# Sparse attention with a routed feed-forward net: transposes of two tokens at once, copies between engines moved, end blocks in 64 columns

## The chip, the cores and the metric

The kernel runs on one core of one Trainium2 chip. A core has engines that work side by side, each through its own queue in order: TensorE (PE, matrix products and transposes, results to PSUM), VectorE (DVE), ScalarE (ACT), GpSimd (POOL) and SyncE (SP, which here only starts transfers). Sixteen DMA engines carry the transfers. The metric is the device time of one execution, in microseconds (us).

## What is computed

Four batches of eight heads with 768 positions and 64 dimensions go through block-sparse attention in blocks of 32 positions. The 3,072 rows that result are then routed to eight experts with 384 places each. The reference, cut to its core:

```python
mask = abs(blk_i - blk_j) <= 1                     # the neighbouring blocks
mask |= (blk_i == 0) | (blk_j == 0) | (blk_i == n_blocks - 1) | (blk_j == n_blocks - 1)
for qb in range(n_blocks):                         # 24 blocks, 3 drawn for each
    for kb in sampled_blocks[qb]:
        mask[32*qb:32*qb+32, 32*kb:32*kb+32] = True
attn = softmax(where(mask, q @ k.T / 8, -1e9))
x = (attn @ v) as rows of 8 heads x 64             # 3072 x 512
logits = x @ w_gate                                # 512 x 8
# all 24576 (token, expert) pairs from the highest logit down: a token goes to the
# first expert with a free place (384 each)
out[rows of e] = relu(x[rows of e] @ w1[e]) @ w2[e]
```

## The kernel before

The program has two parts, one after the other: `Attn` (lines 26 to 462) and `Moe`, whose planner with its own clock places routing and expert products. The change touches `Attn` alone. All numbers are 32-bit floats.

**Layout.** Keys and queries of a batch are needed with the dimension on the partitions: `T[b, "k"]` and `T[b, "q"]`, tiles of 128 x 4 x 768, where partition 64s + d of slice p holds dimension d of head 2p + s. `load_pair` brings them in as `st`, 96 partitions with four neighbouring tokens each, and `prep` (L130) turns them. One call turns two of the four tokens for both heads of a pair: eight products with the identity (L141), each with 64 columns of `st` as weights and 96 moving columns, into one PSUM tile `ptr` or `pT`, and one evacuation with the scale, on ACT (L147) or, for odd places among the first sixteen, on DVE (L149). The evacuation writes every fourth column of `T`. There are sixteen calls in a batch. In the traces a product of 32-bit floats counts as two matmul instructions, a transpose as one.

**Units.** The work of a batch is 24 units in pairs, one for each half s of the heads' partitions. "I" units (20 of them: u = 0 to 4, m, s) handle four middle blocks of queries, u's blocks 4u + 1 to 4u + 4, for two heads; "M" units (2) handle blocks 21 and 22 for four heads; "D" units (4) handle the end blocks, 23 and 0, which attend to all 768 positions. In a batch after the first one D pair comes first and the other after the units of u = 1; then come the rest, and M at the end.

**What a unit goes through.** `qk_pair` (L215) makes the scores of a pair into PSUM tiles `S` (L235; for I and M against gathered keys `kg`, for D against `kT`, four pieces of 32 query columns for every half). `sm_unit` (L237) takes the row minimum (L252, for D L244) and subtracts it (L253 on DVE, for D L247 on ACT). `tr_unit` (L256) transposes the scores (L266) and takes the exponential while it evacuates them (L267, ACT). `av_unit` (L273) multiplies with the value rows (L293 for I and M, from `vw` and `vz`; L280 for D, from `vn`), and `finish` (L298) divides by the sums on DVE. Then come three short tasks, one an iteration: `l1` transposes the attention rows (L342, L344), `l2` multiplies with the gate weights `wp`, padded to 32 columns, into four strips of experts by tokens (L351, L353), and `l3` transposes these (L357) and adds the strips up on DVE into the logits `lg` (L360).

**Gathers.** Each u has its own keys and values in one of two buffers. `gather_k` (L161) fills `kg[u % 2]` with copies: first and last block of the batch (u = 0 and 1 only; L168, L169), the neighbouring blocks (L173, L175, L176 on DVE, in later batches for u = 0 on POOL; L177, L178 on POOL) and the three drawn ones (L182, POOL, twelve copies). `gather_v` (L192) fetches the drawn value rows from DRAM with one indirect transfer for each block (L199, started by POOL) into `vz`, and copies the neighbouring rows from `vn` into `vw` on ACT (L195) and DVE (L202, L210, L212, and memsets L204, L207). `value_frame` (L184) brings the end blocks' rows by transfers of SP.

**Order.** `run` (L364) writes the order of all queues by hand, in a software pipeline. Iteration n issues, in this order: the scores of the pair n + 1 and n + 2 (when n is odd), the products with values of unit n - 3, one task, the transposes of the scores of unit n - 1, stores, then for unit n the softmax step, the gathers and loads that are due, and at the end one `prep` of the next batch. Gathers hang on the place i of a unit in its u:

```python
if i == 3 and u < 4:
    self.gather_k(b, u + 2)
if i == 2:
    self.gather_v(b, u + 1)
```

In M, `gather_k(b + 1, i)` makes both key buffers of the next batch, one for each M unit. `prep` uses the PSUM tile `px`, or, when a D unit is among the last four, one of the two buffers `pT` that the transposes use too.

Of the kernel before, what the change touches and what calls it, by code (L numbers as in the profile page):

```python
# [25 lines left out]
class Attn:  # L26
# [23 lines left out]
    def consts(self):  # L50
        nc, cst = self.nc, self.cst
        sb32 = self.sb.tensor.bitcast(I32)
        self.tab = cst.tile([128, NB, 3, 2], I32, name="tab")
        nc.scalar.dma_start(self.tab.rearrange("p n r w -> p (n r w)"),
                            bass.AP(tensor=sb32, offset=0, ap=[[0, 128], [1, 2 * NB * 3]]))
        self.tbl = cst.tile([128, NB, 3], I32, name="tbl")
        nc.vector.tensor_scalar(self.tbl, self.tab[:, :, :, 0], 0, NB - 1, op0=OP.max, op1=OP.min)
        self.kg = [cst.tile([128, HP, 4, 256], F32, name=f"kg{i}") for i in range(2)]
        self.vw = [cst.tile([128, 4, VR], F32, name=f"vw{i}") for i in range(2)]
        self.vz = [cst.tile([128, 4, VR], F32, name=f"vz{i}") for i in range(2)]  # L60
# [69 lines left out]
    def prep(self, b, p, nm, t, n=None, px=True):  # L130

        nc = self.nc
        if p == 0 and t == 0:
            self.T[b, nm] = self.qk.tile([128, HP, S], F32, name=nm + "T")
        ps = (self.px[:, 0:384] if px
              else self.pA.tile([128, 512], F32, name="pT")[:, 0:384])
        for h in range(2):
            for c in range(2):
                x = 64 * (2 * t + h)
                for s in range(2):  # L140
                    nc.tensor.matmul(ps[64 * s:64 * s + 64, 192 * h + 96 * c:192 * h + 96 * c + 96],  # L141
                                     self.st[b, p, nm][:, c, s, x:x + 64], self.ident[0:96, 0:96], start=True, stop=True)
        dst = self.T[b, nm][:, p].rearrange("d (r x) -> d x r", x=4)[:, 2 * t:2 * t + 2]
        src = ps.rearrange("d (x r) -> d x r", x=2)
        sc = 1.0 if nm == "k" else -0.125
        if n is None or n % 2 == 0:
            nc.scalar.activation(dst, src, AF.Copy, scale=sc)  # L147
        else:
            nc.vector.tensor_scalar(dst, src, sc, None, op0=OP.mult)  # L149
# [11 lines left out]
    def gather_k(self, b, u):  # L161
        nc = self.nc
        kg, kT = self.kg[u % 2], self.T[b, "k"]
        e = nc.gpsimd if b else nc.vector
        if u < 2:
            for g in range(4):
                s = 32 * ((g + 3) % 4)
                e.tensor_copy(kg[:, :, g, s:s + 32], kT[:, :, 0:32])  # L168
            e.tensor_copy(kg[:, :, :, 224:256], kT[:, :, None, S - BS:S].to_broadcast([128, HP, 4, BS]))  # L169
        e = e if u == 0 else nc.vector  # L170
        x = 128 * u
        for g in range(2):
            e.tensor_copy(kg[:, :, g, 32 * g:32 * g + 96], kT[:, :, x + 32 * g:x + 32 * g + 96])  # L173
        if u < 5:
            e.tensor_copy(kg[:, :, 2:4, 96:128], kT[:, :, None, x + 96:x + 128].to_broadcast([128, HP, 2, 32]))  # L175
            e.tensor_copy(kg[:, :, 2:4, 0:32], kT[:, :, None, x + 128:x + 160].to_broadcast([128, HP, 2, 32]))  # L176
            nc.gpsimd.tensor_copy(kg[:, :, 2, 64:96], kT[:, :, x + 64:x + 96])  # L177
            nc.gpsimd.tensor_copy(kg[:, :, 3, 32:64], kT[:, :, x + 160:x + 192])  # L178
        pv = self.sampled(u, ET.Pool)
        for g in range(len(self.blocks(u))):  # L180
            for r in range(3):
                nc.gpsimd.tensor_copy(kg[:, :, g, 128 + 32 * r:160 + 32 * r], kT[:, :, bass.ds(pv[3 * g + r] * BS, BS)])  # L182
# [9 lines left out]
    def gather_v(self, b, u):  # L192
        nc = self.nc
        vw, vz, vn = self.vw[u % 2], self.vz[u % 2], self.vn[b % 2].rearrange("p c h d -> p c (h d)")
        A = lambda o, i: nc.scalar.activation(o, i, AF.Copy)  # L195
        V = nc.vector.tensor_copy
        bl = self.blocks(u)
        for g in range(len(bl)):
            nc.gpsimd.indirect_dma_start(out=vz[0:96, g], out_offset=None, in_=self.vs[b],  # L199
                                         in_offset=bass.IndirectOffsetOnAxis(ap=self.vidx[:, bl[g]:bl[g] + 1], axis=0))  # L200
        A(vw[0:96, 0], vn[0:96, u])
        V(vw[32:64, 1], vn[32:64, u])  # L202
        if u == 0:
            nc.vector.memset(vw[0:32, 0], 0.0)  # L204
        if u == 5:
            A(vw[64:96, 1], vn[64:96, u])
            nc.vector.memset(vw[96:128, 1], 0.0)  # L207
            return
        A(vw[64:128, 1:3], vn[64:128, u, None].to_broadcast([64, 2, VR]))
        V(vw[0:32, 2], vn[0:32, u + 1])  # L210
        A(vw[96:128, 3], vn[96:128, u])
        V(vw[0:64, 3], vn[0:64, u + 1])  # L212


    def qk_pair(self, xs, js=(0, 1)):  # L215
# [6 lines left out]
        kg, bl = self.kg[u % 2], self.blocks(u)  # L222
        for j in js:
            for g in range(4):
                for s, x in enumerate(xs):
                    h = slice(64 * s, 64 * s + 64)
                    if kind == "D":
                        p, i = 2 * x["m"] + g // 2, (NB - 1, 0)[g % 2]
                        o, rhs = x["S"][j][32 * g:32 * g + 32, 0:384], kT[h, p, 384 * j:384 * j + 384]
                    else:  # L230
                        p, gi = (2 * x["m"] + j, g) if kind == "I" else (2 * j + g // 2, g % 2)
                        i = bl[gi]
                        o = x["S"][0][32 * g:32 * g + 32, 256 * j:256 * j + 256]
                        rhs = kg[h, p, gi]
                    nc.tensor.matmul(o, qT[h, p, BS * i:BS * i + BS], rhs, start=True, stop=True)  # L235
# [37 lines left out]
    def av_unit(self, x):  # L273
        nc, b, kind, u, m, s = self.nc, x["b"], x["kind"], x["u"], x["m"], x["half"]
        aT = x["aT"]
        if kind == "D":
            for n in range(6):
                for g in range(4):
                    h = 4 * m + 2 * (g // 2) + s
                    nc.tensor.matmul(self.px[32 * g:32 * g + 32, (D + 1) * s:(D + 1) * (s + 1)], aT[:, n, 32 * g:32 * g + 32],  # L280
                                     self.vn[b % 2][:, n, h], start=n == 0, stop=n == 5)
        else:
            if x["first"]:
                self.av = self.pV.tile([128, 512], F32, name="av")[:, 0:7 * (D + 1)].rearrange("p (h d) -> p h d", h=7)
# [13 lines left out]
    def finish(self, x):  # L298

        nc, b, kind, u = self.nc, x["b"], x["kind"], x["u"]  # L300
        av = self.av if kind != "D" else self.px[:, 0:2 * (D + 1)].rearrange("p (h d) -> p h d", h=2)
        n, f = {"I": (8, 7), "M": (4, 4), "D": (2, 2)}[kind]
        rc = self.wk.tile([128, 8, 1], F32, name="rc")
        nc.vector.tensor_scalar(rc[:, 0:f], av[:, 0:f, D:D + 1], 1e-9, None, op0=OP.add)
        if kind == "I":
            nc.vector.tensor_scalar(rc[:, 7], self.a7[:, D:D + 1], 1e-9, None, op0=OP.add)
        nc.vector.reciprocal(rc[:, 0:n], rc[:, 0:n])
# [30 lines left out]
        def l1():  # L338
# [4 lines left out]
            st["xT"] = self.wk.tile([128, HP, 128], F32, name="xT")  # L343
            nc.scalar.activation(st["xT"], ps, AF.Copy)  # L344

        def l2():
            ps = self.pA.tile([128, 512], F32, name="pT")
            xT = st["xT"]
            for p in range(HP):
                r = xT[:, p, :] if kind == "I" else xT[:, p - p % 2:p - p % 2 + 2, 64 * (p % 2):64 * (p % 2) + 64]  # L350
                nc.tensor.matmul(ps[32 * p:32 * p + 32, 0:128], self.wp[:, p, :], r, start=True, stop=True)  # L351
            st["LT"] = self.wk.tile([128, 128], F32, name="LT")
            nc.scalar.activation(st["LT"], ps[:, 0:128], AF.Copy)  # L353

        def l3():
            ps = self.pA.tile([128, 512], F32, name="pT")
            nc.tensor.transpose(ps[:, 0:128], st["LT"], self.ident)  # L357
            c = b * 6 + u
            for p0, n, c in ((0, 128, c),) if kind == "I" else ((0, 96, c), (96, 32, (c - 6) % NCH)):
                nc.vector.tensor_reduce(self.lg[p0:p0 + n, c], ps[p0:p0 + n, 0:128].rearrange(  # L360
                    "p (c e) -> p e c", c=4)[:, 0:E], axis=AX.X, op=OP.add)
        self.tasks += [l1, l2, l3]

    def run(self, start=None):  # L364
# [16 lines left out]
        flat = [(p, nm, t) for p in range(HP) for nm in "kq" for t in range(2)]  # L381
# [7 lines left out]
        for n in range(N + 3):  # L389
# [32 lines left out]
            if kind == "D":  # L422
# [5 lines left out]
                if i == (2 if b == 0 else 1):  # L428
                    self.gather_v(b, 0)
                    if b == 0:  # L430
# [5 lines left out]
            if kind == "I":  # L436
# [3 lines left out]
                if i == 3 and u < 4:  # L440
                    self.gather_k(b, u + 2)
# [735 lines left out]
```

## Time and profile before

| what | us |
|---|---|
| median of three runs | 786.71 |
| the runs | 780.67 to 787.73 |
| the profiled execution | 787.75 |
| its span, first to last instruction | 786.0 |
| DVE, ACT, POOL busy in the span | 485.1, 388.6, 398.6 |

The three runs differ by 0.9% between them. In the profile, a group names a line of the kernel, an engine, an operation and the tiles (`out<-in`), with the number of its instructions, then the busy time in us and the mean of one in ns, then the engine's idle time before them and what ended it. The view of waits gives, for each engine and line, what was waited for, with the total in us, the number of times and the longest. A line of the timeline gives the start in us from the span's start, the length in us, the engine, and what it did; neighbouring instructions of the same kind are merged, with their count. Windows give the busy time of each engine in a stretch. All instructions of the second part carry L541, which is a helper's line.

### The profile page before, as it was taken

How to read it: one execution, taken by the hardware profiler on the slowest of the kernel's cores; microseconds unless marked ns; L12 is line 12 of the kernel's file. 1: busy time of each engine (PE TensorE's matmuls, PEld its weight loads, DVE VectorE, ACT ScalarE, POOL GpSimd, SP SyncE). 2: the span in 40 equal slices, each digit the busy share in tenths (PEclk: the TensorE clock that was granted, in tenths of full speed). 3: DMA queues.
4: the chain of work that ended last, by engine and by line, in shares of the span. 5: the costliest groups of instructions: out<-in, count | busy, mean ns of one | idle time of the engine just before them, and what ended most of it. 6: DMA issues, size and time to landing. Idle time of an engine off the chain costs nothing. (4 is left out here: it accounts for less than half of the span.)

```text
span 786.0 us, 22329 instructions
## 1 busy us (share of the span) xinstructions
PE 636.2 (81%) x8736; PEld 481.6 (61%) x8736; DVE 485.1 (62%) x1730; ACT 388.6 (49%) x801; POOL 398.6 (51%) x741
## 2 busy tenths in 40 slices
PE   5768886788767978768767218999999999999997
PEld 5545663555544645545445117787878787889895
DVE  3447458473774657657695687868687878743120
ACT  2335553464534646435343427475757565644350
POOL 2275337336363254544440007575757676777671
PEclk9879998899987999869998558999999999999999
DMA  9945724845345673133321025434353535455411
GB/s 207 258 108 122 186 84 125 205 104 140 118 115 132 124 202 118 37 88 89 93 63 50 8 73 182 161 135 167 129 174 122 184 114 200 153 174 178 139 41 41
DMA packets 84865, 101.07 MB, mean 129 GB/s; under 512 B 30724, under 2 KB 61588, under 8 KB 84760
## 3 DMA queue, kind: packets, MB, share of 16 engines
q1 hardware_dynamic: 75104, 69.39, 30.5%
q0 software_dynamic: 9504, 30.18, 13.3%
q8 instruction: 69, 1.13, 0.7%
q14 instruction: 36, 0.29, 0.1%
q10 hardware_dynamic: 152, 0.08, 0.1%
HBM read 76.38 MB, written 18.98 MB: 121 GB/s over the span
## 5 line engine op out<-in xcount | busy, mean ns | idle before, releaser
L541 POOL TENSOR_TENSOR wlo<-raw,whi 128x512 fp32r<-128x512 f32 x128 | 161.6, 1288 | 58.0 <-ACT whi L541 57.3
L199 POOL DMA_INDIRECT vz<-vrows,vidx x88 | 84.1, 956 | 163.9 <-PE pT L293 130.1
L267 ACT ACTIVATE aT<-pT 128x512 f32<-128x512 f32 x88 | 52.6, 597 | 100.8 <-PE pT L266 100.7
L266 PE MATMUL pT<-ident,s 128*128 128x128 f32 x352 | 63.5, 306 | 33.6 <-DVE s L253 26.8
L182 POOL COPY kg<-kT 128x128 f32 x264 | 68.7, 308 | 24.3 <-issue 24.2
L541 PE MATMUL po<-whi,hh 128*128 128x512 f32 x192 | 77.4, 403 | 0.0
L541 PE MATMUL po<-whi,hl 128*128 128x512 f32 x192 | 77.0, 401 | 0.0
L252 DVE TENSOR_REDUCE mn<-S 128x2 f32<-128x512 f32 x88 | 59.8, 680 | 27.5 <-remote 15.7
L541 PE MATMUL po<-wlo,hh 128*128 128x512 f32 x192 | 76.5, 399 | 0.0
L541 ACT ACTIVATE whi<-raw 128x512 fp32r<-128x512 f32 x128 | 74.1, 621 | 0.1
L266 PEld LDWEIGHTS pT<-ident,s 128*128 128x128 f32 x352 | 43.5, 154 | 43.8 <-issue 30.6
L253 DVE TENSOR_TENSOR s<-S,mn 128x512 f32<-128x512 f32 x88 | 60.9, 692 | 10.8 <-PE pT L266 5.9
L293 PE MATMUL av<-vw,aT 128*32 128x65 f32 x1248 | 54.6, 244 | 14.0 <-issue 12.7
L293 PE MATMUL av<-vz,aT 128*32 128x65 f32 x1248 | 54.0, 239 | 14.0 <-issue 13.7
L235 PE MATMUL S<-kg,qT 64*32 64x256 f32 x1408 | 57.6, 401 | 3.9 <-issue 3.8
L541 DVE SCALAR_TENSOR_TENSOR hl<-ph,hh 128x384 fp32r<-128x384 f32 x64 | 35.3, 553 | 39.7 <-ACT hh L541 38.1
L541 PE MATMUL ph<-xhi,whi 128*128 128x384 f32 x256 | 58.4, 345 | 0.4 <-ACT xhi L541 0.3
L293 PEld LDWEIGHTS av<-vw,aT 128*32 128x32 f32 x1248 | 31.5, 118 | 43.9 <-issue 39.7
L541 PE MATMUL ph<-xhi,wlo 128*128 128x384 f32 x256 | 57.9, 343 | 0.0
L541 PE MATMUL ph<-xlo,whi 128*128 128x384 f32 x256 | 57.7, 342 | 0.0
L541 ACT ACTIVATE hh<-ph 128x384 fp32r<-128x384 f32 x64 | 31.2, 487 | 45.5 <-PE ph L541 42.4
L195 ACT ACTIVATE vw<-vn 96x520 f32<-96x520 f32 (+2 forms) x68 | 51.8, 762 | 1.0
(247 smaller groups left out, 1365.2 us busy)
## 6 DMA issues: line engine op xcount, KB each, us to landing
raw<-in_moe_w_dram SPq DMA_DIRECT2D x64, 512.0 KB
stk<-in_k_dram SPq DMA_DIRECT2D x32, 192.0 KB
stq<-in_q_dram SPq DMA_DIRECT2D x32, 192.0 KB
vn<-in_v_dram SPq DMA_DIRECT2D x24, 256.0 KB
xrows<-xt SPq DMA_DIRECT2D x20, 256.0 KB
vrows<-vn SPq DMA_DIRECT2D x9, 520.0 KB
vw<-vn SPq DMA_DIRECT2D x32, 65.0 KB
vz<-vn SPq DMA_DIRECT2D x8, 260.0 KB
```

Source lines behind the costliest of these rows:

```text
L182: nc.gpsimd.tensor_copy(kg[:, :, g, 128 + 32 * r:160 + 32 * r], kT[:, :, bass.ds(pv[3 * g + r] * BS, BS)])
L195: A = lambda o, i: nc.scalar.activation(o, i, AF.Copy)
L199: nc.gpsimd.indirect_dma_start(out=vz[0:96, g], out_offset=None, in_=self.vs[b], in_offset=bass.IndirectOffsetOnAxis(ap=self.vidx[:, bl[g] ...
L235: nc.tensor.matmul(o, qT[h, p, BS * i:BS * i + BS], rhs, start=True, stop=True)
L252: nc.vector.tensor_reduce(mn[:, 0:2], ps, axis=AX.X, op=OP.min)
L253: nc.vector.tensor_tensor(s.rearrange("p (j t) y -> p j (t y)", j=2), ps, mn[:, 0:2, None].to_broadcast([128, 2, 256]), op=OP.subtract)
L266: nc.tensor.transpose(ps[:, c, :], s[:, c0 + c, :], self.ident)
L267: nc.scalar.activation(aT[:, c0:c0 + w], ps[:, 0:w], AF.Exp, scale=-1.0 if n == 4 else 1.0)
L293: nc.tensor.matmul(o(self.col(x, j))[32 * g:32 * g + 32], aT[:, 2 * j + t, 32 * g:32 * g + 32], v[:, gi, h], start=t == 0, stop=t == 1)
L541: return f(*args, **kw)
```

## The change

Six edits, all in `Attn`.

- `prep(b, p, nm, s)` now turns all four tokens of one head: four transposes, each of 128 columns of `st` (two tokens), into 96 columns of the PSUM tile. Its two halves of 64 partitions hold the even and the odd tokens; ACT evacuates the first and DVE the second, each into every second column of `T`.
- The rows that DVE copied from `vn` to `vw` come by transfers of SP, in a new function `copy_v`, called one unit after `gather_v` (in the same unit for u = 0). The memsets go to POOL.
- The neighbouring keys go to POOL (L173) and ACT (L175, L176), also for u = 1 of the first batch; only its u = 0 stays on DVE.
- The end blocks' queries are put side by side by ACT into a new tile `qd`, so that scores and value products of D units take 64 columns at once.
- The logits come as tokens by experts straight from PE: the attention rows are the weights and the gate's eight columns move, added up over four products; ACT copies the result to `lg`. `l3`, its transpose and its addition on DVE go. `l1` of M puts its rows into the order that this needs.
- The sums in `finish` are kept in PSUM (`den`) and not in SBUF before their reciprocal.

```diff
-        wp = cst.tile([128, HP, 32], F32, name="wp")
-        nc.gpsimd.memset(wp, 0.0)
-        nc.gpsimd.dma_start(wp[:, :, 0:E], wg.rearrange("(c p) e -> p c e", p=128))
+        wp = cst.tile([128, HP, E], F32, name="wp")
+        nc.gpsimd.dma_start(wp, wg.rearrange("(c p) e -> p c e", p=128))
...
-        for h in range(2):
-            for c in range(2):
-                x = 64 * (2 * t + h)
-                for s in range(2):
-                    nc.tensor.matmul(ps[64 * s:64 * s + 64, 192 * h + 96 * c:192 * h + 96 * c + 96],
-                                     self.st[b, p, nm][:, c, s, x:x + 64], self.ident[0:96, 0:96], start=True, stop=True)
-        dst = self.T[b, nm][:, p].rearrange("d (r x) -> d x r", x=4)[:, 2 * t:2 * t + 2]
-        src = ps.rearrange("d (x r) -> d x r", x=2)
+        for c in range(2):
+            for t in range(2):
+                x = 192 * c + 96 * t
+                nc.tensor.transpose(ps[:, x:x + 96], self.st[b, p, nm][:, c, s, 128 * t:128 * t + 128], self.ident[0:96, 0:96])
         sc = 1.0 if nm == "k" else -0.125
-        if n is None or n % 2 == 0:
-            nc.scalar.activation(dst, src, AF.Copy, scale=sc)
-        else:
-            nc.vector.tensor_scalar(dst, src, sc, None, op0=OP.mult)
+        for z in range(2):
+            dst = self.T[b, nm][64 * s:64 * s + 64, p, z:S:2].rearrange("d (c r t) -> d c r t", c=2, t=2)
+            src = ps[64 * z:64 * z + 64].rearrange("d (c t r) -> d c r t", c=2, t=2)
+            if z == 0:
+                nc.scalar.activation(dst, src, AF.Copy, scale=sc)
+            else:
+                nc.vector.tensor_scalar(dst, src, sc, None, op0=OP.mult)
...
-        e = nc.gpsimd if b else nc.vector
+        e = nc.gpsimd if b or u else nc.vector
...
-        e = e if u == 0 else nc.vector
         x = 128 * u
         for g in range(2):
             e.tensor_copy(kg[:, :, g, 32 * g:32 * g + 96], kT[:, :, x + 32 * g:x + 32 * g + 96])
         if u < 5:
-            e.tensor_copy(kg[:, :, 2:4, 96:128], kT[:, :, None, x + 96:x + 128].to_broadcast([128, HP, 2, 32]))
-            e.tensor_copy(kg[:, :, 2:4, 0:32], kT[:, :, None, x + 128:x + 160].to_broadcast([128, HP, 2, 32]))
+            nc.scalar.activation(kg[:, :, 2:4, 96:128], kT[:, :, None, x + 96:x + 128].to_broadcast([128, HP, 2, 32]), AF.Copy)
+            nc.scalar.activation(kg[:, :, 2:4, 0:32], kT[:, :, None, x + 128:x + 160].to_broadcast([128, HP, 2, 32]), AF.Copy)
...
-        A(vw[0:96, 0], vn[0:96, u])
-        V(vw[32:64, 1], vn[32:64, u])
         if u == 0:
-            nc.vector.memset(vw[0:32, 0], 0.0)
+            nc.gpsimd.memset(vw[0:32, 0], 0.0)
+            A(vw[32:64, 0], vn[32:64, u])
+            A(vw[64:96, 0], vn[64:96, u])
+        else:
+            A(vw[0:96, 0], vn[0:96, u])
...
+    def copy_v(self, b, u):
+
+        vw, vn = self.vw[u % 2], self.vn[b % 2].rearrange("p c h d -> p c (h d)")
+        D = self.nc.sync.dma_start
+        D(vw[32:64, 1], vn[32:64, u])
+        if u < 5:
+            D(vw[0:32, 2], vn[0:32, u + 1])
+            D(vw[0:64, 3], vn[0:64, u + 1])
...
+        if kind == "D" and 0 in js:
+            p = 2 * xs[0]["m"]
+            for z, i in enumerate((NB - 1, 0)):
+                nc.scalar.activation(self.qd[:, p:p + 2, 32 * z:32 * z + 32], qT[:, p:p + 2, BS * i:BS * i + BS], AF.Copy)
         for j in js:
-            for g in range(4):
+            for g in range(2 if kind == "D" else 4):
...
-                        p, i = 2 * x["m"] + g // 2, (NB - 1, 0)[g % 2]
-                        o, rhs = x["S"][j][32 * g:32 * g + 32, 0:384], kT[h, p, 384 * j:384 * j + 384]
+                        p = 2 * x["m"] + g
+                        o, rhs = x["S"][j][64 * g:64 * g + 64, 0:384], kT[h, p, 384 * j:384 * j + 384]
+                        lhs = self.qd[h, p]
...
-                for g in range(4):
-                    h = 4 * m + 2 * (g // 2) + s
-                    nc.tensor.matmul(self.px[32 * g:32 * g + 32, (D + 1) * s:(D + 1) * (s + 1)], aT[:, n, 32 * g:32 * g + 32],
-                                     self.vn[b % 2][:, n, h], start=n == 0, stop=n == 5)
+                for g in range(2):
+                    nc.tensor.matmul(self.px[64 * g:64 * g + 64, (D + 1) * s:(D + 1) * (s + 1)], aT[:, n, 64 * g:64 * g + 64],
+                                     self.vn[b % 2][:, n, 4 * m + 2 * g + s], start=n == 0, stop=n == 5)
...
-                nc.tensor.matmul(ps[32 * p:32 * p + 32, 0:128], self.wp[:, p, :], r, start=True, stop=True)
-            st["LT"] = self.wk.tile([128, 128], F32, name="LT")
-            nc.scalar.activation(st["LT"], ps[:, 0:128], AF.Copy)
-
-        def l3():
-            ps = self.pA.tile([128, 512], F32, name="pT")
-            nc.tensor.transpose(ps[:, 0:128], st["LT"], self.ident)
-            c = b * 6 + u
+                nc.tensor.matmul(ps, xT[:, p], self.wp[:, p], start=p == 0, stop=p == HP - 1)
             for p0, n, c in ((0, 128, c),) if kind == "I" else ((0, 96, c), (96, 32, (c - 6) % NCH)):
-                nc.vector.tensor_reduce(self.lg[p0:p0 + n, c], ps[p0:p0 + n, 0:128].rearrange(
-                    "p (c e) -> p e c", c=4)[:, 0:E], axis=AX.X, op=OP.add)
-        self.tasks += [l1, l2, l3]
+                nc.scalar.activation(self.lg[p0:p0 + n, c], ps[p0:p0 + n], AF.Copy)
+        self.tasks += [l1, l2]
...
-                if i == 3 and u < 4:
-                    self.gather_k(b, u + 2)
+                if i == 3:
+                    self.copy_v(b, u + 1)
+                    if u < 4:
+                        self.gather_k(b, u + 2)
```

More of the change, by code (lines that the diff above doesn't have):

```diff
@@ L59, in consts @@
         self.vw = [cst.tile([128, 4, VR], F32, name=f"vw{i}") for i in range(2)]
+        self.qd = cst.tile([128, HP, 2 * BS], F32, name="qd")
         self.vz = [cst.tile([128, 4, VR], F32, name=f"vz{i}") for i in range(2)]
@@ L128, in value_rows, with prep @@
                                self.vn[b % 2][:, c:c + n].rearrange("p c h d -> p c (h d)"))
-    def prep(self, b, p, nm, t, n=None, px=True):
+    def prep(self, b, p, nm, s, n=None, px=True):
         nc = self.nc
-        if p == 0 and t == 0:
+        if p == 0 and s == 0:
             self.T[b, nm] = self.qk.tile([128, HP, S], F32, name=nm + "T")
@@ L195, in gather_v @@
         A = lambda o, i: nc.scalar.activation(o, i, AF.Copy)
-        V = nc.vector.tensor_copy
         bl = self.blocks(u)
@@ L301, in finish @@
         av = self.av if kind != "D" else self.px[:, 0:2 * (D + 1)].rearrange("p (h d) -> p h d", h=2)
+        den = self.avt[:, 480:488] if kind != "D" else self.px[:, 480:488]
         n, f = {"I": (8, 7), "M": (4, 4), "D": (2, 2)}[kind]
         rc = self.wk.tile([128, 8, 1], F32, name="rc")
-        nc.vector.tensor_scalar(rc[:, 0:f], av[:, 0:f, D:D + 1], 1e-9, None, op0=OP.add)
+        nc.vector.tensor_scalar(den[:, 0:f, None], av[:, 0:f, D:D + 1], 1e-9, None, op0=OP.add)
         if kind == "I":
-            nc.vector.tensor_scalar(rc[:, 7], self.a7[:, D:D + 1], 1e-9, None, op0=OP.add)
-        nc.vector.reciprocal(rc[:, 0:n], rc[:, 0:n])
+            nc.vector.tensor_scalar(den[:, 7:8], self.a7[:, D:D + 1], 1e-9, None, op0=OP.add)
+        nc.vector.reciprocal(rc[:, 0:n, 0], den[:, 0:n])
         r0 = b * S
@@ L342, in l1 @@
                 nc.tensor.transpose(ps[:, p, :], i_.rearrange("p a d -> p (a d)"), self.ident)
[L343 to L344 removed]
+            st["xT"] = xT = self.wk.tile([128, HP, 128], F32, name="xT")
+            if kind == "I":
+                nc.scalar.activation(xT, ps, AF.Copy)
+            else:
+                for a in (0, 2):
+                    nc.scalar.activation(xT[:, a:a + 2].rearrange("p o (z y) -> p z o y", z=2),
+                                         ps[:, a:a + 2].rearrange("p z (o y) -> p z o y", o=2), AF.Copy)
         def l2():
[L347 to L348 removed]
+            ps = self.pA.tile([128, 512], F32, name="pT")[:, 0:E]
+            xT, c = st["xT"], b * 6 + u
             for p in range(HP):
[L350 to L358 removed]
+                nc.tensor.matmul(ps, xT[:, p], self.wp[:, p], start=p == 0, stop=p == HP - 1)
             for p0, n, c in ((0, 128, c),) if kind == "I" else ((0, 96, c), (96, 32, (c - 6) % NCH)):
[L360 to L362 removed]
+                nc.scalar.activation(self.lg[p0:p0 + n, c], ps[p0:p0 + n], AF.Copy)
+        self.tasks += [l1, l2]
     def run(self, start=None):
@@ L380, in run @@
         N = len(units)
-        flat = [(p, nm, t) for p in range(HP) for nm in "kq" for t in range(2)]
+        flat = [(p, nm, s) for p in range(HP) for nm in "kq" for s in range(2)]
         for i, pr in enumerate(flat[:8]):
@@ L429, in run @@
                     self.gather_v(b, 0)
+                    self.copy_v(b, 0)
                     if b == 0:
```

11 lines of the change are left out of this document (5 added, 6 removed).

## The prediction

> **What bounds the kernel now.** First the page's head and its line of granted clock, then the busy times of three stretches.
>
> ```profile
> span 786.0 us, 22329 instructions
> PEclk9879998899987999869998558999999999999999
> ```
> ```profile
> 0.00:40.00 40.00, 25.90 (x380) 20.46 (x380) 15.59 (x45) 11.82 (x17) 10.35 (x38) 0.91 0.97 232
> 40.00:436.00 396.00, 301.92 (x6655) 202.77 (x6655) 249.40 (x548) 193.40 (x310) 177.68 (x502) 0.90 0.43 114
> 436.00:786.00 350.00, 308.35 (x1702) 258.40 (x1701) 220.09 (x1138) 183.40 (x475) 210.58 (x202) 0.94 0.40 133
> ```
>
> The columns are PE, weight loads, DVE, ACT, POOL, clock, DMA share, GB/s. The first 40 us belong to the DMA engines (0.97 busy). Then attention runs for 396 us, PE busy for 302 of them and no other engine over 63%. The 350 us of routing and experts aren't touched; I leave them as they are. So everything is decided in 40 to 436, where PE paces: what counts is PE's work and its 94 idle us. Who ended that idle time, in the view of waits of that stretch:
>
> ```profile
> PE pT L266 <- DVE s L253: 26.8, 11, 6.8
> PE av L293 <- issue: 26.5, 42, 1.2
> POOL vz L199 <- PE pT L293: 130.1, 18, 10.5
> ```
>
> The 26.8 us for DVE are eleven waits, and three of them are nearly all. The copy of value rows at L202, by its line and its group, then the timeline around one such place:
>
> ```profile
> L202 DVE COPY vw<-vn x24: 421/438/7996, 40.1 to 420.1; 32x520 f32<-32x520 f32 x24
> busy tenths in 40 slices 0000004000040000300000000000000000000000
> ```
> ```profile
> L202 DVE COPY vw<-vn 32x520 f32<-32x520 f32 x24 | 33.4, 1392 | 0.7
> ```
> ```profile
> 224.25 0.99 POOL L168 COPY kg<-kT 128x128 f32<-128x128 f32 x4
> 232.88 2.88 POOL L182 COPY kg<-kT 128x128 f32 x12
> ```
> ```profile
> 224.55 7.99 DVE L202 COPY vw<-vn 32x520 f32<-32x520 f32 x1
> ```
> ```profile
> 234.82 1.08 PE L266 MATMUL pT<-ident,s 128*128 128x128 f32 x4 [6.78 <-DVE s L253]
> ```
>
> A copy of 438 ns takes 7.99 us where POOL, from 224.25 on, copies the next batch's keys without a pause. It happens at the three changes of batch (the digits 4, 4, 3), and costs 33.4 - 24 x 0.438 = 22.9 us of DVE. PE stands for 6.78 us, some 20 in three. PE then runs on at half clock:
>
> ```profile
> 127.70:134.50 6.80, 4.44 (x57) 2.72 (x57) 3.66 (x8) 0.60 (x1) 3.30 (x14) 0.50 0.12 29
> 230.10:240.30 10.20, 5.47 (x85) 3.44 (x89) 7.03 (x10) 1.14 (x2) 5.66 (x22) 0.50 0.31 73
> 332.50:342.70 10.20, 6.19 (x91) 3.98 (x92) 7.03 (x13) 1.19 (x2) 5.02 (x20) 0.50 0.01 2
> ```
>
> **The change, part by part.**
>
> *Value and key copies leave DVE.* L202, L210 and L212 become SP transfers, L173 goes to POOL, L175 and L176 to ACT, the two memsets to POOL. The three stalls need a DVE copy beside POOL's, so they go: **-20 us** (-20 to 0, the other end if POOL or ACT is simply late next). 4.44 + 5.47 + 6.19 = 16.1 us of PE work ran at half clock there; at full clock it is 8 less. I take **-6** (-8 to 0).
>
> Without the stalls PE waits only 26.8 - 20 = 6.8 us for DVE, so the rest of DVE's relief earns little:
>
> ```profile
> L173 DVE COPY kg<-kT 128x384 f32<-128x384 f32 x42 | 18.7, 487 | 0.0
> L210 DVE COPY vw<-vn 32x520 f32<-32x520 f32 x20 | 8.4, 422 | 0.3
> ```
> ```profile
> L147 ACT ACTIVATE qT<-ptr 128x384 f32<-128x384 f32 x19 | 17.1, 901 | 4.7 <-PE ptr L141 4.6
> L149 DVE TENSOR_SCALAR kT<-pT 128x384 f32<-128x384 f32 x3 | 2.5, 841 | 5.4 <-PE pT L141 5.4
> L244 DVE TENSOR_REDUCE mn<-S 128x1 f32<-128x384 f32 x32 | 17.0, 548 | 12.2 <-PE S L235 9.3 <-remote 2.9
> L247 ACT ACTIVATE sD<-S,mn 128x384 f32<-128x384 f32 x32 | 16.8, 579 | 21.3 <-DVE mn L245 13.9 <-issue 5.5 <-DVE rc L304 1.9
> ```
>
> Out of DVE go 24 x 0.44 + 8.4 + as much for L212 + 18.7, some 46 us. In come 64 evacuations of half the partitions, 384 elements each (8 were there already). What one costs is open: today 841 ns on DVE and 901 on ACT, with results written 16 bytes apart, against 548 and 579 for as many elements without such a step. So 35 to 54 us come in. I take a third above the lower ends, as the new step is 8 bytes but PSUM is now read out of order. DVE gets a little lighter: **-3** (-7 to +8, the latter if evacuations delay the softmax behind them). On ACT, 56 evacuations of 901 ns become 64 of 579 to 901, and 40 key copies of 256 elements come in, 0.4 us each (between L353's and L267's rows below); ACT is busy for 193 of 396 us, so nothing on the path, but see the queries below. [...]
>
> POOL gets 36 copies of 384 elements; by L182's rows (0.24 us for 128) they take 0.5 each, 18 us in all, hidden by the 130 us for which it waits for a free `vz`. Were that cover gone, PE would get up to 18 us back. SP gets 64 transfers, 5.6 MB (2,080 bytes a row, 128 rows a `u`) beside 114 GB/s x 396 us = 45 MB. Each is queued behind the store of the same iteration, and what it waits for (the weighted sums of `u` - 1) is over when that store goes. It is due four units later. I cost it at 0. The 26.5 us of "issue" before L293 come where gathers and stores are in flight; with 12% more bytes they could get 7 worse, and with fewer PE instructions better (0; -8 to +7).
>
> *Transposes of two tokens.* Sixteen instructions of 64 columns become four transposes. Start to next start at full clock, in the timeline:
>
> ```profile
> 270.99 0.66 PE L266 MATMUL pT<-ident,s 128*128 128x128 f32 x4
> 271.58 0.88 PE L141 MATMUL ptr<-ident,stk 96*64 96x96 f32 x16
> 272.39 0.32 PE L293 MATMUL av<-vw,aT 128*32 128x65 f32 x8
> 272.98 0.66 PE L266 MATMUL pT<-ident,s 128*128 128x128 f32 x4
> 273.57 0.88 PE L235 MATMUL S<-kT,qT 64*32 64x384 f32 x16
> 274.38 0.32 PE L293 MATMUL av<-vw,aT 128*32 128x65 f32 x8
> ```
> ```profile
> 40.00:435.00 395.00, 46.91 (x768) 36.86 (x768) 0.90 0.44 115
> ```
>
> L141 takes 272.39 - 271.58 = 0.81, four transposes of 128 by 128 take 0.59. With 96 moving columns the new ones lie between 0.59 and 0.59 x 96/128 = 0.44. L141 is busy for 46.9 us of the stretch (last row): at 0.59 it loses 46.9 x 0.22/0.81 = 13, at 0.44 it loses 21. **-17**, in the middle. Those before 40 us hide behind the loads.
>
> *End blocks in 64 columns.* Sixteen score instructions (L235, 0.81) become eight, 48 of L280 become 24. Do strips of 64 cost the same each as strips of 32? L141 has 64-column strips, two side by side: 16 in 0.81, so 102 ns for one strip. Scaled from 96 to 65 moving columns that is 69 ns; 24 of them two abreast make 0.83, no less than now:
>
> ```profile
> 259.59 0.89 PE L280 MATMUL ptr<-vn,aTD 128*32 128x65 f32 x48
> 260.41 0.66 PE L342 MATMUL pT<-ident,xm 128*128 128x128 f32 x4
> ```
>
> 260.41 - 259.59 = 0.82. So **0** (-14 to 0, the end where the number of instructions sets it: half of 16 x 0.82 and 16 x 0.81).
>
> They add a wait: the stacked queries `qd` are copied by ACT when the scores are issued, so PE, in order, waits until ACT has done what lies before it. For the second end pair of a batch that is an exponential and the value copies:
>
> ```profile
> 273.74 0.60 ACT L267 ACTIVATE aT<-pT 128x512 f32<-128x512 f32 x1 [0.28 <-PE pT L266]
> 274.36 2.37 ACT L195 ACTIVATE vw<-vn 96x520 f32<-96x520 f32 x3
> 280.99 0.35 ACT L353 ACTIVATE LT<-pT 128x128 f32<-128x128 f32 x1
> ```
>
> 0.60 + 2.37 + two small copies (no more than twice L353's 0.35; I take 0.5) = 3.5 us, where L235 today starts at 273.57, right behind L266. For the first pair it is the exponential, two key copies and `qd`, about 2.0. Three batches: 3 x 5.5 = 16.5. Some of it falls where PE stands anyway: **+10** (0 to +17).
>
> *Logits by token.* Per chunk, L351 and L357 take from start to start
>
> ```profile
> 194.83 0.40 PE L351 MATMUL pT<-xT,wp 128*32 128x128 f32 x8
> 195.21 0.66 PE L266 MATMUL pT<-ident,s 128*128 128x128 f32 x4
> ```
> ```profile
> 258.08 0.33 PE L357 MATMUL pT<-ident,LT 128*128 128x128 f32 x1
> 258.25 0.60 PE L266 MATMUL pT<-ident,s 128*128 128x128 f32 x4
> ```
>
> 0.38 + 0.17 = 0.55. The new eight load 128 columns each: from 0.4 (as now) to 8 x 0.15 (a 128-column instruction of L266) = 1.2. So -4 to +15 us over 24 chunks; I take +5, and -5 for the step through ACT and PE that goes with L353 and L357: **0**. At the tail of attention one such step less: **-1**.
>
> Sum: -20 - 6 - 3 - 17 + 10 - 1 = -37. The profiled execution took 787.75 us, 1.75 around its span; 1.0 over the median of 786.71. So 787.75 - 37, **750 us**.
>
> **Rivals.**
>
> *The clock gains more (0.22).* A mean clock of 0.90 over 396 us, taken as a mix of 0.50 and 1.00, is 79 us at half speed, which loses 40. If the denser PE halves that, and `qd` hides, another 14 and 10 go: **726**. For it: the page's low digits stand at the stalls. Against: others stand beside "issue" waits, which stay.
>
> *The stall only moves (0.16).* POOL still needs its 8 us per change of batch, ACT has more in front of what PE wants, and PE stands there for the same 20 us: 750 + 20 = **770**. For it: POOL's copies at 224 to 236 come right before its gathers. Against: their keys are due four units later.
>
> *PE falls to half clock more often, and the change isn't faster (0.07).* Matrix products become transposes. [...] Should the half-clock time double from 79 to 158 us, 40 us are lost: 750 + 40 = **790**. It decides from a mean clock of 0.83 in attention on (29 us lost, 779). [...] The trace speaks against a strong form: the slices of 9 in the line of granted clock hold four transposes of L266 in every unit too.
>
> *DMA contention (0.05).* Copies lengthen the "issue" waits by 7 and land late for the first products of some `u`: **765**.
>
> **How the numbers follow.** The forecast has 0.50, its own range 736 to 764. The range must take in 726 and 770 with what is uncertain about them and leaves out 790: 718 to 775. About 1% is what a measurement of this kernel can tell from no change, so faster is below 779: the forecast, the first rival, most of the second and the contention, 0.89. Same takes the upper end of the second and half of the clock's, 0.07; slower 0.04.
>
> **What would show it.** No DVE copy between SBUF tiles over 1 us, and no wait of 6 us for L253: the stall. Four transposes in 0.44 to 0.59, evacuations near 550 to 700 ns on both engines: the transposes. A wait of PE for `qd` of 2 to 4 us, six times or so. A mean clock of 0.91 to 0.94 in attention. Wrong, if PE's idle time at the changes of batch stays, if POOL no longer waits for `vz`, or if the clock falls below 0.85.

## The result and the profile after

The changed kernel takes 760.8 us (median of four runs, 759.21 to 763.35), the kernel before 786.6 in the same series: a ratio of 0.969 (0.963 to 0.975), some 26 us less. The profiled execution took 759.21 us, 28.5 less than the one that the prediction started from. The forecast was 750, the range 718 to 775, faster with 0.89: faster it is, within the range, with some seven tenths of the gain (26 of 37 us).

The page of the changed kernel, and its attention stretch in the view by windows (columns as in the prediction):

```profile
span 757.4 us, 19869 instructions
PEclk9989897899977899999987569999999999999999
```
```profile
40.00:408.00 368.00, 289.54 (x5623) 201.72 (x5621) 199.39 (x421) 189.28 (x373) 190.92 (x548) 0.89 0.55 138
```

Attention is 28 us shorter (408 against 436). PE is busy 12 us less and idle 78 us instead of 94, DVE is busy 50 us less. The granted clock is 0.89, where it was 0.90. The groups of lines that answer to the steps (busy time, mean ns, then idle time ahead of the group and what ended it):

```profile
L277 PE MATMUL pT<-ident,s 128*128 128x128 f32 x352 | 60.3, 298 | 6.3 <-DVE s L264 4.8 <-ACT aT L278 1.1 <-issue 0.2
L367 PE MATMUL pT<-wp,xT 128*128 128x8 f32 x192 | 29.2, 276 | 2.1 <-issue 1.4 <-ACT xT L360 0.5
L246 PE MATMUL S<-kT,qd 64*64 64x384 f32 x96 | 14.5, 683 | 15.6 <-ACT qd L232 8.8 <-ACT vw L193 3.4 <-issue 3.4
L146 ACT ACTIVATE qT<-ptr 64x384 f32<-64x384 f32 x18 | 9.3, 517 | 0.3
L148 DVE TENSOR_SCALAR qT<-ptr 64x384 f32<-64x384 f32 x18 | 10.1, 560 | 21.5 <-ACT qT L146 20.1 <-issue 1.2
```

The wait for DVE's subtraction, 26.8 us before, is 4.8: the stalls are gone. The evacuations take 517 and 560 ns, where they took 901 and 841. Against that stand two rows that cost: the scores of the end blocks wait 15.6 us for the stacked queries `qd` (three waits of 1.8 us and three of 3.4, whatever name the profile gives to what ended them), and the logits (L367) keep PE busy for 29.2 us. The timeline at one of the six waits:

```profile
155.07 0.63 PE L277 MATMUL pT<-ident,s 128*128 128x128 f32 x4
156.28 2.35 ACT L193 ACTIVATE vw<-vn 96x520 f32<-96x520 f32 x3
158.65 0.40 ACT L232 ACTIVATE qd<-qT 128x64 f32<-128x64 f32 x2
159.11 0.88 PE L246 MATMUL S<-kT,qd 64*64 64x384 f32 x8 [3.41 <-ACT vw L193]
```

PE is through at 155.70. The two small copies stand behind three copies of value rows in ACT's queue, and PE goes on at 159.11. New, too, is a wait at the first end pair of batches 1 and 2 (counted from 0). In the view of waits (sum, number, longest), and beside it the largest that is left of the old ones:

```profile
PE av L304 <- issue: 16.2, 24, 1.4
PE pT L277 <- ACT xT L357: 8.3, 2, 4.4
```

The timeline at the second of the two:

```profile
219.55 0.66 PE L354 MATMUL pT<-ident,xt 128*128 128x128 f32 x4
220.56 0.80 PE L277 MATMUL pT<-ident,sD 128*128 128x128 f32 x4 [0.36 <-issue]
222.69 0.92 POOL L196 DMA_INDIRECT vz<-vrows,vidx  x1 [0.30 <-issue]
225.13 0.60 ACT L357 ACTIVATE xT<-pT 128x512 f32<-128x512 f32 x1 [4.15 <-remote]
225.78 0.69 PE L277 MATMUL pT<-ident,sD 128*128 128x128 f32 x2 [4.42 <-ACT xT L357]
```

By its record PE finished the transposes of L354 at 220.21. ACT was free from 220.98 on, yet its L357, which reads these transposes, starts at 225.13: the semaphore update that follows their end stands at 225.07 in the trace, almost five microseconds late. "Remote" says that the profile finds nobody who ended the wait.

### The profile page after: what moved, and what is told of

It is laid out like the page before. It is cut to its first block, busy times and chain, and to the rows that moved or that the text cites. A ratio compares the mean times of both kernels' runs of the same rounds, so it can differ in the third digit from the quotient of the medians.

```text
span 757.4 us, 19869 instructions
## 1 busy us (share of the span) xinstructions
PE 619.6 (82%) x7432; PEld 475.3 (63%) x7432; DVE 436.5 (58%) x1607; ACT 386.8 (51%) x877; POOL 411.5 (54%) x787
## 5 line engine op out<-in xcount | busy, mean ns | idle before, releaser
L196 POOL DMA_INDIRECT vz<-vrows,vidx x88 | 81.6, 927 | 131.8 <-PE pT L304 103.5
L180 POOL COPY kg<-kT 128x128 f32 x264 | 63.6, 289 | 18.2 <-issue 18.2
L277 PE MATMUL pT<-ident,s 128*128 128x128 f32 x352 | 60.3, 298 | 6.3 <-DVE s L264 4.8
L304 PE MATMUL av<-vw,aT 128*32 128x65 f32 x1248 | 52.4, 243 | 15.4 <-issue 12.0
L246 PE MATMUL S<-kg,qT 64*32 64x256 f32 x1408 | 60.5, 434 | 4.0 <-issue 3.7
L304 PEld LDWEIGHTS av<-vw,aT 128*32 128x32 f32 x1248 | 31.2, 117 | 48.0 <-issue 43.5
L304 PE MATMUL av<-vz,aT 128*32 128x65 f32 x1248 | 51.3, 237 | 4.4 <-issue 4.1
L193 ACT ACTIVATE vw<-vn 32x520 f32<-32x520 f32 (+2 forms) x72 | 53.8, 752 | 0.8
```

The lines of the kernel that those rows point to most:

```text
L246: nc.tensor.matmul(o, lhs, rhs, start=True, stop=True)
L277: nc.tensor.transpose(ps[:, c, :], s[:, c0 + c, :], self.ident)
L304: nc.tensor.matmul(o(self.col(x, j))[32 * g:32 * g + 32], aT[:, 2 * j + t, 32 * g:32 * g + 32], v[:, gi, h], start=t == 0, stop=t == 1)
```

## The experiments

Twelve kernels, one of them the changed kernel again, ran in three series, and not all series on the same sort of chip. In two of them the kernel before took 738 us, in the third, as in the result above, 786. Times are compared within a sort. On the first sort single runs of the kernel before go from 725.6 to 744.1, so a few us between two medians tell little there. Line numbers in rows are those of each kernel.

| kernel | us, median | ratio to before (95%) |
|---|---|---|
| *chips where before takes 738* | | |
| copies only | 703.4 | 0.952 (0.947 to 0.957) |
| transposes only, halves on ACT and DVE | 739.7 | 1.004 (0.994 to 1.014) |
| changed, logits undone | 711.2 | 0.961 (0.955 to 0.967) |
| changed, end blocks undone | 695.3 | 0.942 (0.937 to 0.948) |
| changed | 716.7 | 0.973 (0.957 to 0.988) |
| changed, `qd` early | 698.6 | 0.949 (0.935 to 0.963) |
| changed, halves by turns | 711.2 | 0.968 (0.955 to 0.981) |
| changed, fixed value rows | 714.5 | 0.971 (0.957 to 0.985) |
| *chip where before takes 786* | | |
| changed (first series) | 760.8 | 0.969 (0.963 to 0.975) |
| copies and transposes | 752.9 | 0.958 (0.954 to 0.962) |
| the same, halves by turns | 754.7 | 0.963 (0.957 to 0.969) |
| transposes only, halves on ACT | 770.7 | 0.982 (0.978 to 0.986) |
| copies, plain products | 786.4 | 0.999 (0.996 to 1.003) |

**The parts alone.** Copies only: the kernel before with the new `gather_k`, `gather_v`, `copy_v` and their calls, and nothing else.

> The kernel before with one part of the change: the copies of keys and values and the memsets leave DVE for ACT, POOL and SP; transposes, end blocks and logits stay as they were. Theory: the three 8-us DVE copies beside POOL's copies at the changes of batch were the largest single cost, and without them 20 to 29 us go (758 to 767 us against 786.6), with no DVE copy out of SBUF above 1 us left and no idle time of 6 us before L253. Rival: the work is as late on POOL or ACT, and PE stands at the same place for another reason: 775 us or more, with PE's idle time at the changes of batch as before.

It took 703.4, 35 us less (31 to 39 by the interval): more than the theory's upper end, and the rival falls. Of the waits for DVE's subtraction none reaches 6 us any more. The largest wait of PE that is left in attention is at the first end pair of the three later batches. Both in the view of waits, then the place in the timeline of this kernel:

```profile
PE pT L273 <- DVE s L260: 3.3, 5, 1.1
PE pT L273 <- ACT LT L360: 8.6, 3, 2.9
```

```profile
113.71 0.40 PE L358 MATMUL pT<-xT,wp 128*32 128x128 f32 x8
114.69 2.88 ACT L194 ACTIVATE vw<-vn 32x520 f32<-32x520 f32 x4
117.60 0.28 ACT L360 ACTIVATE LT<-pT 128x128 f32<-128x128 f32 x1
117.93 0.44 PE L273 MATMUL pT<-ident,sD 128*128 128x128 f32 x2 [2.88 <-ACT LT L360]
```

and, on the same chip, in that of the next version (transposes only), which has the value copies of the kernel before:

```profile
220.97 2.37 ACT L194 ACTIVATE vw<-vn 96x520 f32<-96x520 f32 x3
223.37 0.28 ACT L352 ACTIVATE LT<-pT 128x128 f32<-128x128 f32 x1
223.70 0.44 PE L265 MATMUL pT<-ident,sD 128*128 128x128 f32 x2 [2.22 <-ACT LT L352]
```

For u = 0 ACT now makes four value copies instead of three. A small evacuation of the logits stands behind them, PE needs its PSUM buffer, and waits 2.88 us instead of 2.22, three times.

Transposes only:

```diff
-for h, c, s: matmul(ps[64*s:64*s+64, ...], st[:, c, s, x:x+64], ident[0:96, 0:96])
+for c, t: transpose(ps[:, x:x+96], st[:, c, s, 128*t:128*t+128], ident[0:96, 0:96])
+for z in range(2): (ACT if z == 0 else DVE) evacuates partitions 64*z to 64*z+63
```

> The kernel before with one part alone: two tokens transposed at once and evacuated by partition halves; the DVE copies, the end blocks and the logits stay. Theory: the group of PE loses some 20 us of busy time (46.9 to 27.3) and the time falls by 15 to 20 us, to 767 to 772. Rival 1: the transposes let the clock fall; then the mean granted clock of the attention stretch is below 0.87 and the time is 775 or more. Rival 2: DVE's half waits for ACT's half each time (61.7 us of DVE idle time in the changed kernel) and PE in its turn for DVE; then less than 10 us go.

No gain to be seen: 739.7 against 738.3. The clock did not fall below the 0.87 of rival 1, it is 0.91 from 40 to 330 us. Over whole runs it is 0.912 to 0.934, and 0.922 to 0.941 for the kernel before on this chip, so a few us of the missing gain may be the clock's. These groups show more:

```profile
L265 PE MATMUL pT<-ident,s 128*128 128x128 f32 x352 | 59.5, 295 | 43.2 <-DVE s L252 33.8 <-DVE qT L148 5.6 <-ACT kT L146 1.3
L140 PE MATMUL ptr<-ident,stq 96*128 96x96 f32 x72 | 10.1, 266 | 11.7 <-DVE qT L148 11.7
L148 DVE TENSOR_SCALAR qT<-ptr 64x384 f32<-64x384 f32 x18 | 10.1, 562 | 2.1 <-ACT qT L146 1.5
```

PE waits 33.8 us for DVE's subtraction and another 17 for DVE's halves of the evacuations, and DVE is hardly kept waiting by ACT (1.5 us in this group, 9.0 in all four groups of its halves, where the changed kernel on this sort of chip has 39.7): it is late itself. That is rival 2's outcome by another way. In the loop of the kernel before all evacuations are ACT's; now every call gives half of one to DVE, which still has its copies. That this is the reason was tried on the other sort of chip, with both halves on ACT:

```diff
-    if z == 0: nc.scalar.activation(dst, src, AF.Copy, scale=sc)
-    else: nc.vector.tensor_scalar(dst, src, sc, None, op0=OP.mult)
+    nc.scalar.activation(dst, src, AF.Copy, scale=sc)
```

> The kernel before with the transposes of two tokens alone, both halves evacuated by ACT, as in the loop of the kernel before, so that DVE gets no work. Theory: alone the transposes were worth nothing because their half on DVE (0.56 us, 48 times) came on top of the copies of the engine that was late already; with ACT they gain 8 to 16 us, 722 to 730 against 738. Rival: they gain nothing because PE has to wait for something else, or because the clock falls: 735 to 742.

770.7 against 786.5, 15.7 us less, as the theory says. Since the two versions ran on different chips, this supports the reason without shutting out the chip.

**What was given back.** The logits of the kernel before, put back into the changed one:

> The changed kernel with the logits as they were before (padded weights, a second evacuation, a transpose and a DVE reduction). Theory: the eight products of 128 loaded columns cost PE 29.2 us against 19.6 for the two old steps, all on the path; undone, 7 to 10 us go: 751 to 754 against 760.8. Rival: PE has enough standing time beside them, or the third step through ACT and PE that comes back costs as much: 759 to 765.

711.2 against 716.7 for the changed kernel, from two chips of the same sort; the intervals overlap, so the 5.5 us are a difference of medians and no more. In the groups of lines PE loses 8 us: the changed kernel, measured again there, has 25.5 us in L367, this one 10.0 and 7.9 in two lines.

```profile
L367 PE MATMUL pT<-wp,xT 128*128 128x8 f32 x192 | 25.5, 259 | 1.0 <-ACT xT L360 0.5 <-ACT xT L357 0.4
L246 PE MATMUL S<-kT,qd 64*64 64x384 f32 x96 | 13.7, 648 | 15.6 <-ACT qd L232 15.6
```
```profile
L364 PE MATMUL pT<-xT,wp 128*32 128x128 f32 x192 | 10.0, 280 | 1.1 <-ACT xT L357 1.1
L370 PE MATMUL pT<-ident,LT 128*128 128x128 f32 x24 | 7.9, 328 | 0.9 <-ACT LT L366 0.9
```

The end blocks of the kernel before in the changed one (four strips of 32 columns straight from `qT`, no `qd`):

> The changed kernel with the end blocks in strips of 32 columns straight from the queries, so with no stacked copy and no wait for it. Theory: the waits of PE for the stacked queries add up to 15.5 us (three of 1.8, three of 3.4, and 64 columns gain nothing), so 10 to 16 us go: 745 to 751 against 760.8. Rival: PE stands at the same places for the gathers or the exponentials anyway, or the narrower strips cost what the wait did: 757 to 763.

695.3, 21 us less than the changed kernel (again two chips of one sort): more than expected. It has the lowest median of all on this sort of chip, 0.942 of before against 0.973. Is it the wait or the 64-column form? The copies were made early:

```diff
-if kind == "D" and 0 in js: copy the two query blocks into qd
+in the iteration after the last query transposes of a head-pair pair: copy them
```

> The changed kernel with the stacked queries copied an iteration after their transposes, many units before the scores that read them; the 64-column form stays. Theory: the price of the new end blocks is the wait for these copies, so most of what undoing them gained comes back, 10 to 15 us below the changed kernel, and no row has PE waiting for the copies. Rival: the 64-column form itself is slower, or PE then stands for the next thing; less than 5 us go.

 

698.6, and all its runs (693.6 to 698.9) lie below all of the changed kernel's (710.3 to 717.4) on the same chip:

```profile
L255 PE MATMUL S<-kT,qd 64*64 64x384 f32 x96 | 10.5, 508 | 0.0
```

The 15.6 us of waiting are gone and 18 us of time with them. In the two profiled executions the granted clock from 40 to 330 us also differs, 0.93 here and 0.90 in the changed kernel, so a part of the 18 may be the clock's. The wider form neither gains nor costs much: 3 us lie between this and the strips of 32, on two chips.

For these comparisons the changed kernel ran again:

> The changed kernel, unaltered. The chip of the first experiments runs the kernel before in 738 us, not in 787, and its traces lack the 3-to-7-us hold-ups of PE that the first two traces have. Theory: there the change is worth the parts that were undone less what they gave back, so 705 to 714 us, 0.955 to 0.967 of before, about 15 us behind the version with the old end blocks. Rival: the change is worth the 0.969 of the first chip or less.

716.7, 21.6 us less than before and 21 behind the version with the old end blocks: the theory's 705 to 714 is missed, and the ratio is that of the first chip. With 35 from the copies, 21 given back by the end blocks and some 5.5 by the logits, the transposes are left with about 13, as a remainder: the interval of the changed kernel alone is 11 us to either side.

**Halves by turns.** DVE's half waits for ACT's (20.1 us in L148's row in the section on the result); the two write alternate columns of one tile. `if z == 0` became `if s == 0`, so that one engine makes both halves.

> The changed kernel with both partition halves of a pair of tokens evacuated by the same engine, ACT and DVE taking turns by head; bytes and instructions per engine stay. Theory: DVE's idle time behind ACT's halves (61.7 us in the changed kernel) goes, the transposes' buffer is free no sooner, and the time falls by 2 to 6 us. Rival: DVE is not late, so the time stays within 2 us; or two evacuations in a row on ACT delay the exponentials and it is 3 us slower.

711.2, with an interval that overlaps the changed kernel's: not shown. On the other sort of chip, on top of copies and transposes:

> The same, and both partition halves of a pair on one engine, ACT and DVE taking turns by head. Theory: DVE no longer waits for ACT's halves, 3 to 6 us less than with the halves split: 682 to 689. Rival: no difference, or ACT's two evacuations in a row hold up an exponential and it is 2 us slower.

754.7 against 752.9, nothing, though DVE no longer waits for ACT's halves. One of the four groups, with the halves split and then by turns:

```profile
L149 DVE TENSOR_SCALAR kT<-ptr 64x384 f32<-64x384 f32 x16 | 9.3, 579 | 18.0 <-ACT kT L147 17.8
```
```profile
L149 DVE TENSOR_SCALAR kT<-ptr 64x384 f32<-64x384 f32 x16 | 9.0, 565 | 7.7 <-PE ptr L141 7.5
```

DVE's idle time behind ACT isn't on the path.

**Copies and transposes together**, that is the changed kernel without its end blocks and its logits:

> The changed kernel with both the old end blocks and the old logits, so the kernel before with the copies off DVE and the transposes of two tokens. Theory: with DVE relieved the transposes are worth some 13 us that they are not worth alone, so 687 to 693 us where before takes 738 and the copies alone leave 703. Rival: they are worth nothing here either, and the gain of undoing the end blocks hides an interplay: 698 or more.

752.9, a ratio of 0.958 (0.954 to 0.962) where the changed kernel has 0.969 (0.963 to 0.975) on that sort of chip. The expected 690 were for the other sort; here the two undone parts return only 8 us, not 27, and this version is the best here. From the transposes on ACT alone (770.7), the copies bring 18, with half of the evacuations going to DVE in the same step.

**Transposes or plain products?** One word of the last kernel was changed:

```diff
-nc.tensor.transpose(ps[:, x:x+96], st[..., 128*t:128*t+128], ident[0:96, 0:96])
+nc.tensor.matmul(ps[:, x:x+96], st[..., 128*t:128*t+128], ident[0:96, 0:96], start=True, stop=True)
```

> As the first of these four, with plain products with the identity in place of the transposes, of the same size and into the same places. Theory of the clock: if transposes do not count as work for the clock, the mean granted clock from 40 to 330 us rises by 0.01 to 0.02, to the 0.95 that the copies alone show, and the time falls by 3 to 6 us as long as four products take no longer than the 0.43 of four transposes. Rival: they count alike, the clock stays within 0.01 and the time follows the duration of the products alone.

786.4: 33 us more, all that the change had gained. The group of the products, with transposes and then with plain products:

```profile
L141 PE MATMUL ptr<-ident,stq 96*128 96x96 f32 x72 | 10.2, 268 | 0.4 <-DVE kT L149 0.4
```
```profile
L141 PE MATMUL ptr<-ident,stq 96*128 96x96 f32 x146 | 22.1, 300 | 0.2
```

A transpose is one record and a product of 32-bit floats is two (x72 and x146 in the rows); over the stretch PE is busy with this line for 58 us against 28 (46.9 in the old form, by the prediction). So the gain is that of the transpose, and two tokens in one product alone would have gained nothing. And the clock, from 40 to 330 us in the view by windows, first with transposes:

```profile
40.00:330.00 290.00, 227.37 (x4686) 146.94 (x4686) 160.24 (x343) 149.87 (x283) 163.09 (x479) 0.89 0.64 157
```
```profile
40.00:330.00 290.00, 237.51 (x4646) 171.09 (x4646) 156.09 (x334) 145.72 (x270) 149.89 (x447) 0.88 0.57 144
```

0.89 and 0.88: the rival holds, and the transposes of this line, 28 of some 230 us of PE's work, don't pull the granted clock down here.

**The late signals.** If the trains of POOL's indirect transfers cause them, other transfers in their place should help:

```diff
-nc.gpsimd.indirect_dma_start(out=vz[0:96, g], in_=vs[b], in_offset=vidx[:, bl[g]])
+nc.sync.dma_start(vz[0:96, g], vs[b][96*g:96*g+96])
```

> The changed kernel with the sampled value rows read as fixed rows by SP instead of by POOL's indirect transfers, so the weighted sums use other rows; bytes and places written are the same. Theory: PE's hold-ups that end about 1 us after each train of indirect transfers come from these trains; where the chip shows them (57 us in all in the first trace) some 30 us go, where it does not, less than 10. Rival: they come from the traffic itself, and the time stays or rises, as SP has 88 more transfers to issue.

714.5 against 716.7, no difference; but on this sort of chip there is nothing to gain, as the last section shows. The cause stays open.

## Why the prediction was right or wrong

**The stalls of DVE: right.** No DVE copy of 8 us is left, the three 6-us waits for the subtraction are gone, and the copies alone are worth 35 us on one sort of chip (-29 with clock and relief in the sum). On the other they bring 18 on top of the transposes. **Half clock, -6: not seen** in the stretch of the first chip, 0.90 before and 0.89 after, and the sign that was named, 0.91 to 0.94, did not come. New waits had taken the place of the old ones. On the other sort a rise goes with the copies: transposes only, which keeps them on DVE, and copies only, on one chip:

```profile
40.00:330.00 290.00, 213.07 (x4990) 142.66 (x4988) 230.88 (x490) 144.61 (x258) 153.97 (x453) 0.91 0.54 140
```
```profile
40.00:330.00 290.00, 249.76 (x6261) 172.23 (x6261) 160.16 (x367) 192.81 (x333) 186.26 (x537) 0.95 0.68 169
```

The 46 us that leave DVE were summed without L175 and L176, 4.7 us each in the stretch, which left it too.

**"On ACT nothing on the path": wrong in one place.** By its 193 busy of 396 us ACT was free; at the start of a batch its copies stood in a row with a step that PE needs. In copies only each of the three later batches lost some 0.7 us by the fourth copy, 2 in all. In the changed kernel PE's waits at this place are no longer than with three copies: 6.8 us in all on the sort of chip where transposes only has 6.7. So the rival "the stall only moves" is worth 2 us at most by way of these copies.

**Transposes, -17: right in size.** PE's busy time fell from 46.9 to 27.3, the lower end that was worked out, and with ACT doing the evacuations the part alone gave 15.7. What the prediction didn't say is that, with half of the evacuations on DVE, this hangs on DVE having been relieved.

**Evacuation: right in direction.** 517 and 560 ns with results 8 bytes apart, where it was 901 and 841 with 16: about the lower ends of 579 (ACT) and 548 (DVE), not a third above. That third was the author's estimate for PSUM read out of order; read here with a step of 384 bytes, PSUM cost nothing that the rows show.

**The wait for `qd`: the mechanism right, the size wrong on one sort of chip.** Six waits were forecast, with 16.5 us worked out, and 15.6 came. On the sort of chip where before takes 738, the step that failed is the discount to 10, "some of it falls where PE stands anyway": it didn't, and without the waits 18 us went. On the sort that the prediction started from no run undoes this part alone; end blocks and logits together return 8 us there, so the discount may have been right or too small. **The 64-column form at 0: right**, within 3 us.

**Logits, 0: mis-sized.** PE went up by about 8 us (25.5 against 17.9), above the +5 that was taken, within its -4 to +15. Whether the step through ACT and PE that was saved pays for it is not settled: the logits' price is 5.5 us, within the error.

**The sum.** On chips where before takes 786, as on the one that the prediction started from, three steps through the table lead from the kernel before to the changed one. Transposes on ACT: -15.7, forecast -17. The copies on top of them: -18, forecast -29 (-20 for the stalls, -6 for the clock, -3 for DVE's relief). End blocks and logits: +8, forecast +10 and 0. So most of what is missing from the forecast gain of 37 is missing at the copies: the term that failed is -6 for the clock, which stayed at 0.90 and 0.89, and with it some 5 us of stalls and relief that no run splits. The steps add up to the whole by construction, the changed kernel was timed in another series, and in another order a step could have another price.

On chips where before takes 738 the same parts are worth -35, about -13, +21 and some +5.5. There the copies gained more than was forecast and the end blocks cost twice as much. That the ratio of the whole is 0.97 on both sorts is therefore luck as far as the parts go. One thing fits the smaller gain of the copies on the first chip: at two changes of batch, where the stalls were, PE now stands for 3.9 and 4.4 us behind late signals. That this is the reason is argued, not shown.

**The rivals.** "PE falls to half clock more often" falls: the granted clock from 40 to 330 us was 0.89 with transposes and 0.88 with plain products. No run shows the doubled half-clock time behind its 790: the 0.89 over the 368 us of attention, taken as the same mix of 0.50 and 1.00, is some 81 us, against 79 before. "The clock gains more" didn't come on the first chip; on the other sort the copies alone go with 0.95. DMA contention: PE's waits with no cause in the profile before L304 are 16.2 us where L293 had 26.5 (and 8.3 under the name of L357), so in sum the added transfers didn't lengthen them.

## What to carry to other kernels

A small copy that PE waits for belongs in a queue long before its reader, not where the reader is issued; count the instructions ahead of it and take the whole sum as its price until a run shows less, as busy shares say nothing about it. A part of a change can be worth nothing until another part frees the engine that it loads, so try parts alone and in pairs, on the same chip: here the same copies were worth 35 us on one sort and 18 on the other. And where a change brings several parts, undo each: here the copies and transposes without the rest beat the whole.

## What the hardware showed besides

The two sorts of chips differ in one thing that the traces show: how late PE's completions are signalled. For every PE instruction from 40 us on, up to the last product with value rows, the trace has its end and the next update of the semaphore that it signals. Adding up the delays above 0.8 us, each late update once with its longest delay, gives 57 to 72 us for five kernels on chips of 786 us (before 72, changed 57), 37 for the plain products, and 0 to 7 for all eight kernels on those of 738 us. The two times of the kernel before are 48 us apart; how much of the delays lies on the path isn't shown. Most of the long ones end 0.8 to 2 us after a train of POOL's indirect transfers (222.69 + 0.92 and 225.07 above). The same place in the changed kernel, on the other sort of chip, with the same train (the transfer of 202.44 is one of four):

```profile
200.58 0.66 PE L354 MATMUL pT<-ident,xt 128*128 128x128 f32 x4
202.06 0.60 ACT L357 ACTIVATE xT<-pT 128x512 f32<-128x512 f32 x1
202.44 0.92 POOL L196 DMA_INDIRECT vz<-vrows,vidx  x1 [0.31 <-PE pT L277]
202.71 0.44 PE L277 MATMUL pT<-ident,sD 128*128 128x128 f32 x2 [0.16 <-ACT xT L357]
```

In the groups of lines such delays are the "remote" waits of DVE's row minimum, 12.3 us in the changed kernel on the first chip and none on the other:

```profile
L263 DVE TENSOR_REDUCE mn<-S 128x2 f32<-128x512 f32 x88 | 60.3, 686 | 36.9 <-PE S L246 23.7 <-remote 12.3
```
```profile
L263 DVE TENSOR_REDUCE mn<-S 128x2 f32<-128x512 f32 x88 | 60.2, 685 | 26.5 <-PE S L246 25.6
```

What makes these chips differ was not found: the kernel with fixed rows ran only on a chip without the delays.
